# One pool of PSUM banks for the attention's products, 128-row products in the feature transform, and another instruction order

## The chip, the cores and the metric

The kernel runs on one core of a Trainium2 chip. The metric is the device time of one execution in microseconds (us), as a median of runs. TensorE (PE) multiplies, VectorE (DVE), ScalarE (ACT) and GpSimd (POOL) work element by element, SyncE (SP) issues most of the DMA transfers. PSUM, where TensorE's products arrive, has eight banks.

## The reference

Three stages follow each other, in fp32.

```python
# 1. attention: batch 4, heads 8, 768 steps, head size 40
for t in range(S):
    y[:, :, t] = einsum('bhd,bhde->bhe', rt, state)
    Sa = einsum('bhde,bhe->bhd', state, at)
    state = state * wt - einsum('bhd,bhe->bhde', Sa, bt) + einsum('bhd,bhe->bhde', vt, kt)
# 2. x = y as (4, 768, 320)
mixed = real(fft(fft(x, axis=1), axis=2)); u = x + mixed
un = (u - mean(u)) / sqrt(var(u) + 1e-6)
x = u + maximum(un @ w_ch1, 0) @ w_ch2                    # 320 -> 1280 -> 320
# 3.
h = maximum(x.T @ w_tok1, 0) @ w_tok2; u = x + h.T         # 768 -> 256 -> 768
out = u + maximum(u @ v1, 0) @ v2                          # 320 -> 1536 -> 320
```

## The kernel before, in words

**Attention** (class `Attn`). The 768 steps are cut into 12 chunks of 64 steps; 33 heads (one of them empty) lie in 11 groups of three. For each chunk VectorE makes running products of the decay (`decay`, scans at L293 and L296, reciprocal L295), TensorE makes `kg` (L328: products of the `k` and `b` rows with the masked `a` rows, 11 per chunk), and pairs of chunks go through the inversion of a triangular matrix on VectorE (`inv`, L366 to L381). The blocks for it are gathered through DRAM (`Gd`, then `N`), and its results go out to DRAM (`Md`, `Ad`) and come back turned round (`Mst`, `AT`). `merge` joins two half blocks by 32x32 products (`mg` L408, `mc` L418). Then the chain of a chunk runs on TensorE: `x` (L467), `z` (L479), `s` (L499); `s` makes the state with which the next chunk's `x` works. Off this chain lie `kbt` (L430) and `pt` (L447), turned copies of inputs, and the outputs: `zt` (L531), `st` (L523), `sc` (L538) and `y` (L556, L560). Each product lands in a PSUM bank, and ScalarE or VectorE copies it out (ScalarE's copies all have line 250).

**PSUM in the attention.** The eight banks are in five pools: `c` has two (chain and merge), `m` two (`kg`, `sc`), `t` two (turned copies), `y` one, `i` one (inversion). A product takes a bank of its pool and gives it back when its last copy is done.

**Feature transform.** The FFTs are products with tables. `fft` (L906, tile `psA`) goes along the steps, `fft2` (L929, tile `mix`) along the features. `fft2` has four groups per batch entry, 16 in all. Each group adds eight products in one bank: two of 384 columns and six of 192. Operands are split in a high and a low part; in `A[4]` the high part lies in partitions 0 to 63 and the low part in 64 to 127. The product with table 2 uses all 128 rows, the product with table 3 only the upper 64.

**MLPs.** For six blocks of 512 rows each, products `hps` (L998) and `acc` (L988) run over 10 hidden tiles in the first MLP and 12 in the second. `tok` and `tok2` (L1062, L1075) are the products along the steps.

**The order.** The kernel describes all work as operations with an engine, a cost, operands and banks. A planner (`emit`) puts them in an order: of the operations that can start soon it takes the one with the least due time; due times come from the costs, scaled by `SLACK`, plus a table of offsets `OFF` by stage and chunk. Each engine's order is fixed by that. Where the planner expects TensorE to wait for some time and a bank is free, it puts in fillers (`warm`, L59): products of a 128x128 identity that nobody reads. `HT` and the `cols` of an operation enter the planner's picture of TensorE's clock.

Of the kernel before, what the change touches and what calls it, by code (L numbers as in the profile page):

```python
# [19 lines left out]
NG,NH,D,L=11,33,40,64  # L20
NSC=768//L
T0,PERIOD=60,23.502442205459097
SLACK=453.4035
# [4 lines left out]
BANKS={'c': 2, 'm': 2, 't': 2, 'y': 1, 'i': 1}  # L28
YB='y'
# [181 lines left out]
class Attn:  # L211
# [107 lines left out]
    def kg(s,i):  # L319
# [3 lines left out]
        for g in range(0,NG,2):  # L323
            m=min(2,NG-g); w=192*m; h=s.psum('m',[128,512],"kg"); kp=('ps',h[0])
# [69 lines left out]
    def merge(s,i):  # L394
# [122 lines left out]
    def outp(s,i):  # L517
        nc=s.nc; P=s.P; LT=s.LT[i%2]; VZ=s.VZt; VZd=s.VZd; Sbd=s.Sbd; kbt=s.kbt[i%2]
        if i>0:
            h=s.psum('t',[128,512],"st"); kp=('ps',h[0])  # L520
# [6 lines left out]
        for g in range(0,NG,8):  # L527
            m=min(8,NG-g); hz=s.psum('t',[128,512],"zt"); kz=('ps',hz[0])
# [5 lines left out]
        for k in range(6):  # L534
            gs=(k,k+6) if k<5 else (k,); m=len(gs); hs=s.psum('m',[128,512],"sc"); ks=('ps',hs[0]); j=k%4; t=s.sc[j]
# [106 lines left out]
    def plan(s):  # L642
# [9 lines left out]
        s.P.op('NONE',0.0,lambda: None,pools=('y','t','m','c','i'))  # L652
# [16 lines left out]
OFF={'chain': -10683.5, ('chain', 0): -15631.6, ('chain', 1): -14799.7, ('chain', 10): 132022.4, ('chain', 11): 126346.1, ('chain', 2): -6299.2, ('chain', 3): -1037.2,  # L669
     ('chain', 4): 31922.7, ('chain', 5): 33526.1, ('chain', 6): 102034.8, ('chain', 7): 77429.7, ('chain', 8): 99749.8, ('chain', 9): 136807.5, 'dec2': -83569.5,  # L670
     ('dec2', 0): 207815.1, 'decay': -28442.6, ('decay', 0): -171758.2, ('decay', 1): -191635.0, ('decay', 10): 49032.8, ('decay', 11): 134393.3, ('decay', 2): -155857.3,
     ('decay', 3): -148976.4, ('decay', 4): -120978.7, ('decay', 5): 248332.4, ('decay', 6): -3537.5, ('decay', 7): 17076.9, ('decay', 8): 33468.6, ('decay', 9): 64147.4,
     'decode': 78098.6, ('decode', 0): 97303.6, 'fft': -34228.3, ('fft', 0): 157557.4, ('fft', 1): 148470.3, ('fft', 2): 199138.1, ('fft', 3): 189570.1,
     'fft2': -189107.1, ('fft2', 0): 311427.7, ('fft2', 1): 305214.4, ('fft2', 2): 353071.8, ('fft2', 3): 326784.8, 'inv': 58199.8, ('inv', 0): -246768.8,
     ('inv', 1): -80145.3, ('inv', 2): -56157.9, ('inv', 3): 18838.4, ('inv', 4): 54864.3, ('inv', 5): 54651.3, 'kbts': -115839.5, ('kbts', 0): -98283.9,
     ('kbts', 1): -98753.2, ('kbts', 10): 237625.0, ('kbts', 11): 239311.4, ('kbts', 2): 89305.9, ('kbts', 3): 103517.9, ('kbts', 4): 106114.8, ('kbts', 5): 137322.4,
     ('kbts', 6): 139123.4, ('kbts', 7): 199511.0, ('kbts', 8): 202633.2, ('kbts', 9): 224923.8, 'kg': -316699.4, ('kg', 0): 117017.4, ('kg', 1): 115337.6,
     ('kg', 10): 406897.7, ('kg', 11): 373952.9, ('kg', 2): 132794.7, ('kg', 3): 483438.3, ('kg', 4): 519031.2, ('kg', 5): 291674.5, ('kg', 6): 288959.4,
     ('kg', 7): 309931.9, ('kg', 8): 332304.5, ('kg', 9): 344543.4, 'load': -326373.5, ('load', 0): -39494.0, ('load', 1): 117623.2, ('load', 10): 338619.2,
     ('load', 11): 398123.7, ('load', 2): 115743.5, ('load', 3): 122285.7, ('load', 4): 112986.4, ('load', 5): 488502.3, ('load', 6): 478545.2, ('load', 7): 528238.0,  # L680
# [4 lines left out]
     'loada': -20378.0, ('loada', 0): -199541.7, ('loada', 1): -186254.8, ('loada', 10): 90123.2, ('loada', 11): 126291.1, ('loada', 2): -215592.5, ('loada', 3): -236036.9,  # L685
     ('loada', 4): 26756.8, ('loada', 5): 25194.9, ('loada', 6): 59786.8, ('loada', 7): 43065.6, ('loada', 8): 31025.7, ('loada', 9): 107881.0, 'merge': -133126.0,
     ('merge', 0): 302099.7, ('merge', 1): 296292.3, ('merge', 10): 276058.7, ('merge', 11): 274600.3, ('merge', 2): 105949.9, ('merge', 3): 133851.1, ('merge', 4): 151075.7,
     ('merge', 5): 149103.5, ('merge', 6): 220409.7, ('merge', 7): 222091.3, ('merge', 8): 248803.0, ('merge', 9): 242420.5, 'mlp': 37490.7, ('mlp', 0): 82923.3,
     ('mlp', 1): 140446.2, ('mlp', 10): 68410.7, ('mlp', 11): 66917.3, ('mlp', 2): -28738.2, ('mlp', 3): -39724.0, ('mlp', 4): 17549.8, ('mlp', 5): 147878.1,
     ('mlp', 6): 139739.8, ('mlp', 7): -8987.9, ('mlp', 8): 106168.0, ('mlp', 9): 82297.4, 'out_tile': 112459.4, ('out_tile', None): 28626.2, 'outp': -59596.5,  # L690
     ('outp', 0): 34493.1, ('outp', 1): 32964.5, ('outp', 10): 185593.1, ('outp', 11): 182730.1, ('outp', 2): 44389.6, ('outp', 3): 78826.9, ('outp', 4): 76975.8,
     ('outp', 5): 143298.3, ('outp', 6): 148343.4, ('outp', 7): 149927.6, ('outp', 8): 184311.6, ('outp', 9): 183929.4, 'pad': 66629.8, ('pad', 0): 52240.0,
# [488 lines left out]
```

## Time and profile before

| | us |
|---|---|
| median of 3 runs (lowest, highest) | 992.51 (989.52, 996.26) |
| profiled execution | 985.89 |
| its span, first to last instruction | 984.2 |
| TensorE busy | 956.7 |
| VectorE busy | 601.0 |
| ScalarE busy | 409.8 |
| GpSimd busy | 307.5 |

The span is the time on the chip between the first and the last instruction of the profiled execution; the profile's rows are from that execution. Busy time of TensorE counts the time from a product's start to its end in the pipeline, so products that overlap count once. PEld is TensorE's loading of weights, which goes on beside its products. A product of plain fp32 operands stands in the trace as two records for `kg`, `sc`, `x`, `y`, `mg` and the fillers among others. A wait is named by the instruction that ended it.

### The profile page before, as it was taken

To read this page: it belongs to the slowest core of one execution; us is meant where nothing else is said; L and a number is where in the kernel's file an instruction comes from. 1 tells how busy PE (TensorE), PEld (TensorE's weight loads), DVE (VectorE), ACT (ScalarE), POOL (GpSimd) and SP (SyncE) were. 2 spreads that over 40 slices of the span, in tenths; PEclk is the share of its full clock that TensorE was granted. 3 is DMA by queue.
4 is the path that set the end of the run, shared out by engine and by line. 5 is a ranking of instruction groups with operands and counts; after the bars stand their busy time and mean duration, and the time that the engine had idled before them with its cause. 6 is when DMAs were issued, how large, how long until landed. Compare 5 with 4: busy or idle time off the path is not lost.

```text
span 984.2 us, 23552 instructions
## 1 busy us (share of the span) xinstructions
PE 956.7 (97%) x9681; PEld 862.7 (88%) x9681; DVE 601.0 (61%) x1300; ACT 409.8 (42%) x830; POOL 307.5 (31%) x426
## 2 busy tenths in 40 slices
PE   9898999999899899999999999999999999999998
PEld 8898888888798788889888889899999898988987
DVE  5699679798888349989687646756244231312222
ACT  4366777877777465424343222324212121211111
POOL 6746437846743354021305433450000000000000
PEclk9999999999999899999999999999999999999999
DMA  9976679998786987251505553466000000000000
GB/s 226 192 180 157 153 189 219 189 224 201 192 193 164 218 234 249 104 156 43 161 17 178 155 156 106 157 222 232 1 1 28 1 27 1 27 1 28 1 28 27
DMA packets 128663, 123.93 MB, mean 126 GB/s; under 512 B 85119, under 2 KB 106059, under 8 KB 128555
## 3 DMA queue, kind: packets, MB, share of 16 engines
q1 hardware_dynamic: 123803, 100.39, 39.8%
q0 software_dynamic: 4752, 22.03, 6.5%
q8 instruction: 76, 1.25, 0.6%
q14 instruction: 32, 0.26, 0.1%
HBM read 83.76 MB, written 33.85 MB: 120 GB/s over the span
## 4 chain that ended last, share of the span: by engine, by line
PE 75%; DVE 11%; DMA 6%; POOL 3%; issue 2%; ACT 2%; SPq 1%; POOLq 0%; ACTq 0%; DVEq 0%
PE hps L998 24%; PE acc L988 22%; PE sc L538 4%; DVE pr L366 3%; PE kg L328 2%; PE warm L59 2%; PE mix L929 2%; PE tps L1062 2%; PE t2ps L1075 2%; PE y L560 2%; PE psA L906 2%; DVE Mt L367 2%; PE y L556 1%; PE trp L969 1%; DMA Mst<-Md 1%
## 5 line engine op out<-in xcount | busy, mean ns | idle before, releaser
L1001 DVE SCALAR_TENSOR_TENSOR hl<-hps,hh 128x512 fp32r<-128x512 f32 x132 | 91.1, 690 | 228.6 <-ACT hh L1000 228.4
L1000 ACT ACTIVATE hh<-hps 128x512 fp32r<-128x512 f32 x132 | 78.9, 598 | 322.7 <-PE hps L998 322.5
L998 PE MATMUL hps<-th,v 128*128 128x512 f32 x432 | 135.2, 396 | 0.0
L988 PE MATMUL acc<-v,hh 128*128 128x320 f32 x576 | 128.6, 310 | 0.0
L998 PE MATMUL hps<-th,W 128*128 128x512 f32 x360 | 112.5, 396 | 0.4 <-DVE th L974 0.3
L988 PE MATMUL acc<-W,hh 128*128 128x320 f32 x480 | 107.6, 311 | 0.0
L988 PEld LDWEIGHTS acc<-v,hh 128*128 128x128 f32 x576 | 98.4, 188 | 5.1
L852 POOL TENSOR_TENSOR mda<-mda,mdh 128x320 f32<-128x320 f32 (+2 forms) x44 | 45.3, 1042 | 183.1 <-DVE mdt L850 159.2
L998 PEld LDWEIGHTS hps<-th,v 128*128 128x128 f32 x432 | 81.1, 188 | 16.7
L988 PE MATMUL acc<-v,hl 128*128 128x320 f32 x288 | 88.9, 309 | 0.0
L59 PE MATMUL warm<-ident 128*128 128x128 f32 x664 | 85.6, 283 | 2.0 <-POOL Q L254 2.0
L988 PEld LDWEIGHTS acc<-W,hh 128*128 128x128 f32 x480 | 81.6, 188 | 3.7
L59 PEld LDWEIGHTS warm<-ident 128*128 128x128 f32 x664 | 79.7, 196 | 3.6 <-POOL Q L254 2.0
L998 PEld LDWEIGHTS hps<-th,W 128*128 128x128 f32 x360 | 67.7, 188 | 14.8 <-PE trp L969 0.5
L988 PE MATMUL acc<-W,hl 128*128 128x320 f32 x240 | 74.3, 310 | 0.3 <-DVE hl L1001 0.3
L998 PE MATMUL hps<-tl,v 128*128 128x512 f32 x144 | 57.0, 396 | 0.0
L538 PE MATMUL sc<-rm,VZd 120*128 120x192 f32 x264 | 54.9, 342 | 1.9 <-DVE sc L543 1.0
L988 PEld LDWEIGHTS acc<-v,hl 128*128 128x128 f32 x288 | 54.1, 188 | 0.0
L328 PE MATMUL kg<-am,bt 120*128 120x192 f32 x242 | 50.7, 353 | 3.2 <-ACT am L250 2.3
L328 PEld LDWEIGHTS kg<-am,bt 120*128 120x128 f32 x242 | 41.2, 201 | 7.7 <-POOL bt L305 2.5
L998 PE MATMUL hps<-tl,W 128*128 128x512 f32 x120 | 47.3, 394 | 0.0
L538 PEld LDWEIGHTS sc<-rm,VZd 120*128 120x128 f32 x264 | 41.6, 189 | 6.3 <-DVE sc L543 2.6
(179 smaller groups left out, 1947.8 us busy)
## 6 DMA issues: line engine op xcount, KB each, us to landing
bt<-in_bkR_dram SPq DMA_DIRECT2D x12, 660.0 KB
mdraw<-in_moe_w_ch_dram SPq DMA_DIRECT2D x22, 320.0 KB
wS<-in_wR_dram SPq DMA_DIRECT2D x12, 335.2 KB
a<-in_aR_dram SPq DMA_DIRECT2D x12, 335.2 KB
RT<-a SPq DMA_DIRECT2D x36, 111.7 KB
LT<-in_vT_dram SPq DMA_DIRECT2D x12, 330.0 KB
VZt<-in_vT_dram SPq DMA_DIRECT2D x12, 330.0 KB
r<-in_rR_dram SPq DMA_DIRECT2D x12, 330.0 KB
```

Source lines behind the costliest of these rows:

```text
L59: for x in range(m): nc.tensor.matmul(t[:,128*(x%4):128*(x%4)+128],lhsT=ident,rhs=ident,start=True,stop=True)
L328: nc.tensor.matmul(ps[:,192*x:192*x+192],lhsT=bt[:,g+x].rearrange("p v t -> p (v t)"),rhs=am[:,:,g+x],start=True,stop=True)
L366: P.op('DVE',(.02+.0022*st[0]*shape[0]) if shape[0]==4 and shape[1]<8 else (.048+.00108*st[0]*shape[0]),lambda: V.tensor_tensor(out=pr,in0 ...
L367: P.op('DVE',c,lambda: V.tensor_reduce(out=ev(o),in_=pr,axis=AX.X,op=ALU.add),[('pr',h)],wr)
L538: for x,g in enumerate(gs): nc.tensor.matmul(ps[:,192*x:192*x+192],lhsT=VZd[:,g].rearrange("p v t -> p (v t)"),rhs=s.rm[:,:,g],start=True, ...
L560: nc.tensor.matmul(ps[64*x:64*x+64,c:c+40],lhsT=t[:,3*x+hh],rhs=kbt[:,3*g+hh],start=i==0,stop=True,skip_group_check=True)
L852: P.op('POOL',.06+d*.0025,lambda: nc.gpsimd.tensor_tensor(out=g("da").bitcast(F32),in0=g("da").bitcast(F32),in1=g("dh").bitcast(F32),op=AL ...
L906: nc.tensor.matmul(ps[:,c0:c0+cn],lhsT=t[xx][:,k,o:o+128],rhs=s.at.T1[:,r,tb,c0:c0+cn],start=n==0 and g==0,stop=n==len(seq)-1 and g==len(G)-1)
L988: nc.tensor.matmul(s.pst(acc[x]),lhsT=a[:,sl],rhs=t[w2][w][:,m],start=(m==0 and n==0),stop=(m==MT-1 and n==2))
L998: for n,(l,r) in enumerate(ops): nc.tensor.matmul(ps,lhsT=l,rhs=r,start=n==0,stop=n==7)
L1000: s.act(512,lambda: nc.scalar.activation(out=t["hh"][z],in_=s.pst(h),func=AF.Relu),[kp],[('hh',z)],free=[h[0]])
L1001: s.dve(.61,lambda: nc.vector.scalar_tensor_tensor(out=t["hl"][z],in0=s.pst(h),scalar=0.0,in1=t["hh"][z].bitcast(F32),op0=ALU.max,op1=ALU. ...
```

## The change

All products of the attention take their bank from one pool `c` of seven banks; `i` keeps one. In the transform along the features the product with table 3 uses all 128 rows; the lower half of table 3, zero before, now repeats its upper half. The `cols` of the two 32x32 products of `merge` are 307 instead of 512, `HT` is 3550 instead of 3300, `SLACK` 1446.5 instead of 453.4, and the whole table `OFF` has other numbers (the diff shows a line of it).

```diff
-SLACK=453.4035
+SLACK=1446.5000
-BANKS={'c': 2, 'm': 2, 't': 2, 'y': 1, 'i': 1}
-YB='y'
+BANKS={'c': 7, 'i': 1}
+YB='c'
...
-            m=min(2,NG-g); w=192*m; h=s.psum('m',[128,512],"kg"); kp=('ps',h[0])
+            m=min(2,NG-g); w=192*m; h=s.psum('c',[128,512],"kg"); kp=('ps',h[0])
...
-            P.op('PE',.255,f,[('B',i%4),('AT',i%4)]+([kp+(0,)] if k else []),[kp+(k,),('T',32),('T',96)],alloc=h[0] if k==0 else None,cols=512,ni=32,q='D')
+            P.op('PE',.255,f,[('B',i%4),('AT',i%4)]+([kp+(0,)] if k else []),[kp+(k,),('T',32),('T',96)],alloc=h[0] if k==0 else None,cols=307,ni=32,q='D')
...
-            h=s.psum('t',[128,512],name); kp=('ps',h[0])
+            h=s.psum('c',[128,512],name); kp=('ps',h[0])
...
-            gs=(k,k+6) if k<5 else (k,); m=len(gs); hs=s.psum('m',[128,512],"sc"); ks=('ps',hs[0]); j=k%4; t=s.sc[j]
+            gs=(k,k+6) if k<5 else (k,); m=len(gs); hs=s.psum('c',[128,512],"sc"); ks=('ps',hs[0]); j=k%4; t=s.sc[j]
...
-OFF={'chain': -10683.5, ('chain', 0): -15631.6, ('chain', 1): -14799.7, ('chain', 10): 132022.4, ('chain', 11): 126346.1, ('chain', 2): -6299.2, ('chain', 3): -1037.2,
+OFF={'chain': -74749.0, ('chain', 0): 150606.4, ('chain', 1): 226254.3, ('chain', 10): 223225.9, ('chain', 11): 231718.6, ('chain', 2): -17036.4, ('chain', 3): 110610.3,
...
-HT=3300.0
+HT=3550.0
...
-    T2[64:,2]=T2[:64,2]
+    T2[64:,2:]=T2[:64,2:]
...
-                ops=[(A[4],2,128,W),(A[4],3,64,W)]+[y for e in range(2) for y in ((A[2*e],0,128,E[e]),(A[2*e],1,128,E[e]),(A[2*e+1],0,128,E[e]))]
+                ops=[(A[4],2,128,W),(A[4],3,128,W)]+[y for e in range(2) for y in ((A[2*e],0,128,E[e]),(A[2*e],1,128,E[e]),(A[2*e+1],0,128,E[e]))]
```

**First place: TensorE, from behind the first chunk's `x` to the first `mc`.** `kg` names the chunk by its operand (`bt_124`, `bt_125` and `bt_122` are chunks 2, 3 and 4). Before:

```order
L328 MATMUL kg<-am_117,bt_124 128x192 x11
L59 MATMUL warm<-ident 128x128 x19
L328 MATMUL kg<-am_117,bt_125 128x192 x4
L59 MATMUL warm<-ident 128x128 x2
L328 MATMUL kg<-am_117,bt_125 128x192 x4
L59 MATMUL warm<-ident 128x128
L328 MATMUL kg<-am_117,bt_125 128x192 x3
L59 MATMUL warm<-ident 128x128 x54
L328 MATMUL kg<-am_117,bt_122 128x192 x11
L59 MATMUL warm<-ident 128x128 x11
L408 MATMUL mg<-AT_145,B_146 32x32 x32
L59 MATMUL warm<-ident 128x128 x6
```

With the change:

```order
L328 MATMUL kg<-am_117,bt_124 128x192 x11
L59 MATMUL warm<-ident 128x128 x19
L328 MATMUL kg<-am_117,bt_125 128x192 x11
L59 MATMUL warm<-ident 128x128 x69
L328 MATMUL kg<-am_117,bt_122 128x192 x11
L408 MATMUL mg<-AT_145,B_146 32x32 x32
L59 MATMUL warm<-ident 128x128 x14
L418 MATMUL mc<-Mst_143,T_147 32x32 x32
```

The products are the same; the fillers go from 93 to 102 here, and `mg` follows `kg` directly.

**Second place: the queue of SP and VectorE around the first inversion.** `Gd_157` takes the blocks of chunks 0 and 1 (`RT_131`, `RT_132`), `N_118` reads them back, `wS` and `bt` are loads for later chunks. SP before:

```order
L248 DMA Gd_157<-RT_131 32x32x32 x2
L248 DMA bt_122<-in_bkR_dram 120x1408
L248 DMA bt_125<-in_bkR_dram 120x1408
L248 DMA RT_131<-a_115 40x715 x3
L248 DMA Gd_157<-RT_132 32x32x32 x2
L248 DMA wS_110<-in_wR_dram 120x715
L248 DMA N_118<-Gd_157 64x1024
L248 DMA a_115<-in_aR_dram 120x715
L248 DMA RT_132<-a_116 40x715 x3
L248 DMA N_118<-Gd_157 64x1024
```

With the change:

```order
L248 DMA bt_125<-in_bkR_dram 120x1408
L248 DMA Gd_157<-RT_131 32x32x32 x2
L248 DMA VZd_141<-in_vR_dram 120x11x64
L248 DMA r_138<-in_rR_dram 120x704
L248 DMA N_118<-Gd_157 64x1024
L248 DMA Gd_157<-RT_132 32x32x32 x2
L248 DMA RT_131<-a_115 40x715 x3
L248 DMA wS_110<-in_wR_dram 120x715
L248 DMA N_118<-Gd_157 64x1024
```

The second `N` now stands behind three `RT` and one `wS` after `Gd`, without the load of `a_115` and the three `RT_132`. On VectorE, inside the inversion (`Mt`, `pr`, `it`), there stood before:

```order
L366 TENSOR_TENSOR pr_121<-N_118,it 128x512 x2
L367 TENSOR_REDUCE it<-pr_121 128x8x8 x2
L366 TENSOR_TENSOR pr_121<-Mt_119,it 128x512 x2
L367 TENSOR_REDUCE Mt_119<-pr_121 128x8x8 x2
L381 COPY it<-Mt_119 128x256
```

And with the change:

```order
L367 TENSOR_REDUCE it<-pr_121 128x8x8 x2
L366 TENSOR_TENSOR pr_121<-Mt_119,it 128x512 x2
L367 TENSOR_REDUCE Mt_119<-pr_121 128x8x8 x2
L293 SCALAR_TENSOR_TENSOR Q_112<-wS_111,D_113 120x715
L295 RECIPROCAL D_114<-Q_112 120x11
L296 SCALAR_TENSOR_TENSOR R_126<-wS_111,D_114 120x715
L381 COPY it<-Mt_119 128x256
```

The two scans and the reciprocal of chunk 5 moved into the inversion; a reciprocal and a scan of chunk 4 (`R_130`), which stood ahead of it, moved in as well, near its start.

**Third place: TensorE around the chain of chunk 5.** Before:

```order
L479 MATMUL z<-bdX_142,Mst_144 64x80 x16
L430 MATMUL kbt<-ident,bt_124 128x120 x4
L328 MATMUL kg<-am_117,bt_123 128x192 x4
L430 MATMUL kbt<-ident,bt_124 128x120 x4
L328 MATMUL kg<-am_117,bt_123 128x192 x4
L430 MATMUL kbt<-ident,bt_124 128x120 x3
L328 MATMUL kg<-am_117,bt_123 128x192 x3
L499 MATMUL s<-VZt_137,kbt_149 40x40 x33
L531 MATMUL zt<-ident,VZt_137 120x64 x11
L59 MATMUL warm<-ident 128x128 x10
L467 MATMUL x<-LT_135,RT_133 64x40 x32
```

With the change:

```order
L328 MATMUL kg<-am_117,bt_123 128x192 x11
L408 MATMUL mg<-AT_145,B_146 32x32 x32
L59 MATMUL warm<-ident 128x128 x10
L418 MATMUL mc<-Mst_144,T_147 32x32 x32
L59 MATMUL warm<-ident 128x128 x5
L479 MATMUL z<-bdX_142,Mst_144 64x80 x16
L59 MATMUL warm<-ident 128x128 x5
L499 MATMUL s<-VZt_137,kbt_149 40x40 x33
L531 MATMUL zt<-ident,VZt_137 120x64 x11
L59 MATMUL warm<-ident 128x128 x5
L538 MATMUL sc<-rm_140,VZd_141 128x192 x6
```

`kbt` and `kg` products, which stood between `z` and `s`, stand ahead of `mg`; between the links of the chain there are fillers.

## Rows read from the trace of the kernel before

**Rows 1.** The page's head: span, then busy us, share and instructions of each engine.

```profile
span 984.2 us, 23552 instructions
...
PE 956.7 (97%) x9681; PEld 862.7 (88%) x9681; DVE 601.0 (61%) x1300; ACT 409.8 (42%) x830; POOL 307.5 (31%) x426
```

**Rows 2.** By stretch: length, busy time of each engine, clock, DMA share, GB/s.

```profile
0.00:75.00 75.00, 69.94 (x592) 67.65 (x593) 54.60 (x81) 36.58 (x56) 46.46 (x71) 0.98 0.86 201
75.00:390.00 315.00, 298.38 (x5666) 264.81 (x5664) 244.89 (x538) 218.83 (x437) 174.44 (x260) 0.98 0.81 196
390.00:425.00 35.00, 33.34 (x224) 28.45 (x223) 32.30 (x100) 15.97 (x51) 3.91 (x4) 1.00 0.41 145
425.00:984.20 559.20, 555.01 (x3206) 501.80 (x3205) 269.25 (x583) 138.46 (x290) 82.65 (x92) 1.00 0.23 75
```

**Rows 3.** TensorE's waits from 75 to 390: us in total, times, longest.

```profile
PE mc L418 <- ACT T L250: 4.0, 2, 3.7
...
PE pt L447 <- ACT kbt L250: 1.1, 1, 1.1
```

**Rows 4.** Timeline of TensorE: start, length, instructions; fillers and what follows.

```profile
63.85 12.22 PE L59 MATMUL warm<-ident 128*128 128x128 f32 x108
...
75.91 4.45 PE L328 MATMUL kg<-am,bt 120*128 120x192 f32 x22
```

**Rows 5.** Groups by form; a wait of the weight loads; pieces of the chain.

```profile
L929 PE MATMUL mix<-T,A 64*128 64x384 f32 x16 | 7.0, 438 | 0.0
...
L929 PEld LDWEIGHTS mix<-T,A 64*128 64x128 f32 x16 | 2.9, 183 | 3.5 <-issue 3.5
...
PEld mix L929 <- issue: 6.5, 32, 0.3
...
425.87 1.87 PE hps L998 x8
...
430.90 2.79 PE mix L929 x16
...
491.64 4.02 PE psA L906 x36
```

**Rows 6.** Timeline of TensorE at 120 us: `mg` and what follows it.

```profile
120.51 0.44 PE L408 MATMUL mg<-AT,B 32*32 32x32 f32 x16
120.88 0.63 PE L430 MATMUL kbt<-ident,bt 120*128 120x120 f32 x4
121.44 0.95 PE L408 MATMUL mg<-AT,B 32*32 32x32 f32 x48
122.32 0.53 PE L430 MATMUL kbt<-ident,bt 120*128 120x120 f32 x3
```

**Rows 7.** Groups by form: weight loads of `sc` and `kg`, idle time before them.

```profile
L538 PEld LDWEIGHTS sc<-rm,VZd 120*128 120x128 f32 x264 | 41.6, 189 | 6.3 <-DVE sc L543 2.6 <-issue 0.9 <-ACT sc L250 0.9
L328 PEld LDWEIGHTS kg<-am,bt 120*128 120x128 f32 x242 | 41.2, 201 | 7.7 <-POOL bt L305 2.5 <-ACT RT L250 1.8 <-issue 1.8
```

**Rows 8.** Pieces of the chain, 0 to 80 us: start, length, what.

```profile
30.37 7.62 DMA Gd<-RT
...
40.41 6.50 DMA N<-Gd
```

**Rows 9.** Timeline of VectorE: a scan, a reciprocal, the inversion's first and last.

```profile
35.12 1.65 DVE L293 TENSOR_TENSOR_SCAN Q<-wS,D 120x715 f32<-120x715 f32 x1 [5.28 <-POOL R L299]
36.80 0.23 DVE L295 RECIPROCAL D<-Q 120x11 f32<-120x11 f32 x1
...
47.41 0.17 DVE L369 COPY Mt<-it 128x4 f32<-128x4 f32 x1 [0.97 <-ACT it L368]
...
69.22 1.21 DVE L367 TENSOR_REDUCE Mt<-pr 128x32 f32<-128x512 f32 x2
```

**Rows 10.** A piece of the chain, and the stretch behind it (columns of rows 2).

```profile
317.53 11.29 DMA AT<-Ad
...
336.35:343.15 6.80, 6.62 (x164) 6.33 (x166) 1.16 (x4) 3.01 (x7) 0.86 (x1) 0.50 0.71 193
```

More of the change, by code (lines that the diff above doesn't have):

```diff
@@ L418, in f @@
                     nc.tensor.matmul(ps[p:p+32,n//2],lhsT=s.T[p+32:p+64,n//2],rhs=Mst[p+32:p+64,n//2,32:64],start=True,stop=True,skip_group_check=True)
-            P.op('PE',.255,f,[('T',32),('T',96)]+D+([kq+(0,)] if k else []),[kq+(k,),('Mst',x,2)],alloc=g[0] if k==0 else None,cols=512,ni=32,q='D')
+            P.op('PE',.255,f,[('T',32),('T',96)]+D+([kq+(0,)] if k else []),[kq+(k,),('Mst',x,2)],alloc=g[0] if k==0 else None,cols=307,ni=32,q='D')
         for p in (0,64):
@@ L443, in pts @@
             gs=[(k-k0,x,k+6*x) for k in range(k0,k0+kn) for x in range(2) if k+6*x<NG]
-            h=s.psum('t',[128,512],"pt"); kp=('ps',h[0])
+            h=s.psum('c',[128,512],"pt"); kp=('ps',h[0])
             def f(gs=gs,h=h):
@@ L519, in outp @@
         if i>0:
-            h=s.psum('t',[128,512],"st"); kp=('ps',h[0])
+            h=s.psum('c',[128,512],"st"); kp=('ps',h[0])
             def f():
@@ L527, in outp @@
         for g in range(0,NG,8):
-            m=min(8,NG-g); hz=s.psum('t',[128,512],"zt"); kz=('ps',hz[0])
+            m=min(8,NG-g); hz=s.psum('c',[128,512],"zt"); kz=('ps',hz[0])
             def f(g=g,m=m,hz=hz):
@@ L651, in plan @@
         s.P.filler=lambda b,j,m: warm(s.nc,s.ps[b][j],s.ident,m)
-        s.P.op('NONE',0.0,lambda: None,pools=('y','t','m','c','i'))
+        s.P.op('NONE',0.0,lambda: None,pools=('c', 'i'))
         go(0,'load'); s.init(); go(0,'decay','kg','loada'); s.init2(); first(1); s.init3()
@@ L668 @@
 BL=2.761166073747128
-OFF={'chain': -10683.5, ('chain', 0): -15631.6, ('chain', 1): -14799.7, ('chain', 10): 132022.4, ('chain', 11): 126346.1, ('chain', 2): -6299.2, ('chain', 3): -1037.2,
[L670 to L680, printed above, removed]
[4 rows of a table removed]
[L685 to L692, printed above, removed]
-     'pts': -65642.9, ('pts', 0): -153885.4, ('pts', 1): 39076.5, ('pts', 10): 190183.7, ('pts', 11): 178987.4, ('pts', 2): 58178.1, ('pts', 3): 53924.8,
-     ('pts', 4): 85782.3, ('pts', 5): 85106.6, ('pts', 6): 153334.9, ('pts', 7): 143312.5, ('pts', 8): 151428.5, ('pts', 9): 188736.7, 'tok': -290701.5,
-     ('tok', 0): 472044.2, ('tok', 1): 464667.7, ('tok', 2): 437332.8, ('tok', 3): 428210.6, 'tok2': -443306.7, ('tok2', 0): 679101.0, ('tok2', 1): 602125.0,
-     ('tok2', 2): 565845.0, ('tok2', 3): 417967.0, 'wdec': 108931.7, ('wdec', 0): 35575.6, ('wdec', 1): 38674.8, ('wdec', 10): -299.7, ('wdec', 11): 4844.7,
-     ('wdec', 2): -152569.0, ('wdec', 3): -138466.9, ('wdec', 4): -102678.7, ('wdec', 5): -100979.8, ('wdec', 6): -31010.7, ('wdec', 7): -25950.9, ('wdec', 8): -46380.3,
-     ('wdec', 9): -2547.4}
@@ L1114, in finish @@
         for x in (s.m3s,s.w2s,s.left,s.k2s): x.close()
-PA=('c','c','i')
+PA=('c', 'c', 'i')
 TM=343.0758349479737
```

25 lines of the change are left out of this document (added), and 8 rows, old and new, of the table OFF.

## The prediction

> **What bounds the kernel now.** I read the page's first section, then the busy time by stretch, then the waits of TensorE. TensorE is busy for 956.7 of 984.2 us [rows 1], so the sum below is made in TensorE time, and the reader is to see where that time could shrink. By stretches [rows 2] there are two regimes. From 425 us to the end TensorE is busy for 555.0 of 559.2 us: the two MLPs stream product after product and whatever is taken from a product there comes off the end. In the 390 us before, TensorE sits idle for 5.1 us (0 to 75) and 16.6 us (75 to 390), while VectorE is busy for 245 of the 315 us, ScalarE for 219 and the DMA engines for 81%. No engine fills that stretch; it is held together by waits of one engine for another. The fillers (`warm`, products of the identity whose result nobody reads) stand where the plan expected TensorE to wait. The longest TensorE wait named there is 4.0 us for the evacuation of `mg` [rows 3].
>
> The profiled execution took 985.89 us for a span of 984.2 (1.7 around it); the median of the runs is 992.51, 0.7% above. I make the sum against 984.2 and move the median by the same number of microseconds.
>
> **The change, part by part.**
>
> *Fillers.* Counted in the two orders, TensorE's products other than fillers are the same 6397; the fillers grow from 332 to 408. Each is two records. From the first of 108 records to the product behind them pass 75.91 - 63.85 = 12.06 us [rows 4], so a filler costs 0.223 us. By place: ahead of the first `mc` 219 become 244 (+25, 5.6 us); from there to the first `mix` 84 become 140 (+56, 12.5 us); after that 29 become 24 (-5, -1.1 us). All 76 together are 17.0 us. They cost that if TensorE has work it could do instead, and nothing where it would have waited anyway.
>
> *The 64-row product.* Each of the 16 groups of `mix` has eight products, of which one has 64 rows. Two groups take 2.79 us, so one takes 1.395 [rows 5]. What should it take? A product of 512 columns takes 1.87/8 = 0.233 us (`hps`), one of 192 takes 4.02/36 = 0.112 (`psA`), and one of 384, by its columns, 0.174. Two of 384 and six of 192 make 1.02 us. So 0.375 us a group goes elsewhere, and the row of the weight loads says where: they sat idle 32 times, twice in each of 16 groups, for 6.5 us in total, and waited for nothing that the profile shows [rows 5]. Half of it stands before the 64-row load itself (3.5 us over 16). I read this as the price of going to 64 rows and back. With 128 rows in all eight, 16 x 0.375 = 6.0 us go. Twelve of the groups stand between MLP products, where TensorE never waits, and come off the end in full (4.5 us). The first four stand ahead of the first MLP product, on the path to it, but with fillers beside them; I count them too. Bounds: 0, if the second 384-column product is slow for another reason, and 6.5, the idle time itself. I take 6.0. The extra 64 rows add no columns, and the table's lower half is filled on the host into the same transfer.
>
> The Trainium skill, "TensorEngine Tiling (Array Packing)", Tiling Modes (Key Properties), says that going from one tiling mode to another drains the engine; the 0.2 us beside each of the 32 loads agrees. Against it, "TensorE: Matmul & The Clock Gate", Part 2 (LDWEIGHTS), says that a load's time goes with its columns and that the row count doesn't matter; by that alone the edit is worth nothing and the sum ends 6 us higher, which is the third rival below.
>
> *Changes of shape.* The attention's products come in four shapes (128 or 120 rows by 120 or 128 columns; fewer columns; 40 or 64 rows; 32 by 32). Eight `mg` products and the change behind them take 120.88 - 120.51 = 0.37 us, 24 of them 122.32 - 121.44 = 0.88 [rows 6]; so a product takes 0.032 and the change 0.115. In the order before TensorE goes from shape to shape 229 times, in the new one 208 times: -21 x 0.12 = -2.5 us.
>
> *One pool of banks.* `kg` and `sc` shared two banks and now share seven with everything else. What this can give is the time that their weight loads waited for an evacuation [rows 7]: for `kg` 1.8 us (ScalarE's `RT`), for `sc` 2.6 (VectorE) and 0.9 (ScalarE), 5.3 us; with the 1.1 us that `pt` waited for `kbt`'s evacuation among TensorE's waits, 6.4. Bounds 0 and 6.4. I take half of 5.3, -2.7, because the evacuations are no faster and later products still need their results.
>
> *The new order, start.* The first `mc` waits for the first inversion, and that for `N`. Before, its last transfer is issued at 40.41 us and takes 6.5 [rows 8]; between the landing of `Gd` (37.99) and that issue SP's queue spent 2.4 us on three `RT` transfers and what lay between. In the new order these three and the load of `wS` stand ahead while `Gd` is under way, so `N` may leave at once: -2.4 us, up to -5 with two loads fewer ahead of it. Against this, VectorE now does three scans and two reciprocals inside the inversion, which took from 47.41 to 70.43 us by itself [rows 9]: 3 x 1.65 + 2 x 0.23 = 5.4 us. Behind the inversion, `AT` is issued with one load between it and the writing of `Ad`, where before five transfers lay between. I put the start at +1.0 us, between -2 and +5.6 (all its fillers).
>
> *The new order, attention.* Fillers +12.5 us. The third order fence shows why: the chain `mg`, `mc`, `z`, `s`, `zt` of one chunk, which had `kg` and `kbt` products between its links, now has fillers between them. They take TensorE time, but some of it is time in which it waited before: of 16.6 us idle [rows 2], I let a third of the new fillers, 4.2 us, stand in such waits, for the plan foresees only a part of them. It does not foresee the worst: the transfer of `AT` that took 11.3 us, behind which TensorE then ran for 6.8 us at a granted clock of 0.50 [rows 10], 1.2 GHz instead of 2.4. In the new queue a load of `VZd` again stands ahead of that `AT`.
>
> Sum: -6.0 (64 rows) +1.0 (start) +12.5 -4.2 (fillers in the attention) -2.5 (shapes) -2.7 (banks) -1.1 (fillers later) = -3.0 us. The profiled span would be 981.2, the median 989.5.
>
> **The rivals.**
>
> *The fillers simply add.* If TensorE's waits in the attention stay as long as they are (they are set by landings and evacuations, not by banks), the fillers come on top: +5.6 +12.5 -1.1 -2.5 -6.0 = +8.5 us, 1001.0. For it speaks that in the new order dependent products stand closer (the `z` of the last chunk directly behind its `x`), so that a late evacuation is no longer hidden. It decides from the point where TensorE, between 75 and 390 us of work, still idles 16 us or more.
>
> *The waits go.* If the shared banks give their full 6.4 us, half of the new fillers stand in old waits (another -2.1) and the late `AT` of 317 us is in time (4.0 us of wait and half of 6.8 us at half clock, -7.4), the sum is -3.0 -3.7 -2.1 -7.4 = -16 us, 976.
>
> *The doubled rows bring nothing.* Then -3.0 + 6.0 = +3.0, 995.5. Against it speaks the idle time before exactly those loads.
>
> **How the numbers follow.** My forecast (982 to 998 by itself) has a chance of 0.50, fillers that add (998 to 1008) 0.25, waits that go (970 to 982) 0.19, rows that bring nothing 0.06. The predicted time is 989.5. The range from 976 to 1004 leaves out about 0.1 on each side. About 1% (9.9 us) is what a measurement of this kernel can tell from no change. Faster by over 1% (below 982.6) takes the third case and a little of the first: 0.23. Slower by over 1% (above 1002.4) takes under the better half of the fillers that add, and a little of the late start: 0.17. The rest, 0.60, is within 1%.
>
> **What would show it.** `mix` groups of about 1.0 us, and weight loads there without idle time, show the 6.0 us right; groups of 1.4 us show it wrong. The first `mc` starts at 85.4 us now; at 84 to 88 the start is as I put it. Idle time of TensorE from 75 to 390 us near 10 us, with some 30 us of fillers there, shows the fillers in waits; idle of 16 us or more shows that they added. The first `hps` starts at 416.0 us now; it should start at about 417.5 (the sum without the twelve groups behind it), and from there to the end 4.5 us less than the 568.2 of now should pass. The forecast is wrong above all if the late transfers of the attention come at other places: a wait of 4 us costs its half clock as well.

## The result and the profile after

The changed kernel takes 980.33 us (median of 4 runs, 973.90 to 983.35) beside 991.01 us for the kernel before on the same chip: a ratio of 0.9894, with a 95% interval of 0.9853 to 0.9935. The forecast was 989.5, range 976 to 1004, most of the chance on "within 1%". The range holds the time; the forecast itself was 9 us too long, and the change came out at the edge between "same" and "faster by 1%". The experiments brought nineteen more runs of the changed kernel and, beside them and the others, 96 of the kernel before. The means of the 23 and of the 96 are 981.7 and 990.3 us, so the change is worth **-8.6 us (95%: 1.7 either way)**, where the sum had -3.0.

The page of the changed kernel begins with its span, and then the busy time of each engine (answers to [rows 1]):

```profile
span 972.2 us, 23884 instructions
...
PE 952.2 (98%) x9833; PEld 873.1 (90%) x9833; DVE 604.3 (62%) x1300; ACT 409.9 (42%) x830; POOL 305.8 (31%) x426
```

By stretch, in the columns of [rows 2]:

```profile
0.00:75.00 75.00, 71.35 (x627) 69.97 (x628) 53.51 (x82) 34.66 (x52) 50.54 (x73) 1.00 0.89 203
75.00:390.00 315.00, 304.65 (x5826) 278.36 (x5825) 248.37 (x555) 225.34 (x457) 168.54 (x255) 0.99 0.82 203
390.00:425.00 35.00, 33.07 (x219) 29.50 (x218) 32.79 (x97) 13.32 (x36) 9.31 (x10) 1.00 0.31 97
425.00:972.20 547.20, 543.14 (x3168) 495.32 (x3166) 269.65 (x571) 136.58 (x287) 77.39 (x88) 1.00 0.23 76
```

TensorE idles for 10.4 us between 75 and 390 us, where it idled for 16.6 [rows 2]. What it still waits for there (total, times, longest; answers to [rows 3]):

```profile
PE kg L328 <- POOL bt L305: 2.1, 2, 1.0
PE y L560 <- POOL sc L548: 1.5, 2, 0.8
PE s L499 <- ACT VZt L250: 1.5, 2, 0.9
PE mc L418 <- issue: 1.4, 2, 1.3
```

The wait of 4.0 us of `mc` for `T` is gone, and nothing longer than 1.3 us stands in its place in this profile; two more profiles of the changed kernel have waits of up to 2.4 us (`s` for `VZt`), and none of `mc` for `T`. The forms of `mix` and the weight loads of `sc` and `kg` (answers to [rows 5, 7]):

```profile
L538 PEld LDWEIGHTS sc<-rm,VZd 120*128 120x128 f32 x264 | 42.0, 190 | 1.3 <-issue 0.2
L328 PEld LDWEIGHTS kg<-am,bt 120*128 120x128 f32 x242 | 39.0, 190 | 3.8 <-POOL bt L305 2.5 <-ACT am L250 0.8 <-issue 0.2
...
L929 PEld LDWEIGHTS mix<-T,A 128*128 128x128 f32 x128 | 17.6, 190 | 2.1 <-issue 0.7 <-ACT DE L932 0.7 <-DVE tl L973 0.5
...
L929 PE MATMUL mix<-T,A 128*128 128x384 f32 x32 | 8.6, 350 | 1.2 <-DVE DE L933 0.7 <-DVE tl L973 0.3 <-issue 0.2
```

There is no form of 64 rows any more, and the 6.5 us in which the weight loads of `mix` waited for nothing are 0.7. The weight loads of `sc` and `kg` idle for 5.1 us where they idled for 14.0. In the chain of waits, one group of `mix` takes 1.01 us (eight products in the first line), where it took 1.395 [rows 5]:

```profile
430.01 1.01 PE mix L929 x8
431.01 1.88 PE hps L998 x8
434.66 2.02 PE mix L929 x16
```

**How the runs are compared.** The two profiled executions are 12.0 us apart in span (984.2 and 972.2), the means of all runs only 8.6. What the two profiles have on top is mostly TensorE's clock. The profile after has a mean granted clock of 0.998, about the highest of its 23 runs (their mean is 0.9917); the profile before has 0.991, where the mean of its 96 runs is 0.9877. In the stretches below 1, TensorE is granted 1.2 GHz in place of 2.4, as in [rows 10]. They come and go from execution to execution of one and the same kernel. Every run lists its span and its mean clock, so the two can be put beside each other: over the 221 runs of all kernels here, each kernel against its own mean, a clock lower by 0.001 goes with a span longer by 0.785 us (0.065 either way). A clock lower by 0.001 means about 2 us more at half speed, which would cost 1 us if TensorE were all that counts, so four fifths of it is paid. With that slope each kernel's mean span splits into a span at full clock and a part that the clock costs. The runs come from several chips; at full clock the kernel before takes between 978.5 and 979.2 us on each of the four that ran the experiments, so they are put together. The split is an estimate: differences of spans at full clock are good to about 1 to 1.8 us, and to 2.5 to 2.8 for the two kernels without fillers, whose clocks (0.951 to 0.962) lie below those of all other runs (0.976 to 0.998), so that the slope is carried beyond most of what it was measured on. Seven more runs, each over 1.5% longer than the fastest of its kernel, are left out of the slope and the table; with them the slope is 0.84 us.

| kernel | runs | mean us | mean clock | span at full clock, us |
|---|---|---|---|---|
| before | 96 | 990.3 | 0.9877 | 978.9 |
| changed | 23 | 981.7 | 0.9917 | 973.5 |
| mix128_b | 12 | 984.8 | 0.9878 | 973.6 |
| mix64_a | 10 | 987.0 | 0.9914 | 978.5 |
| pool_b | 11 | 987.9 | 0.9869 | 975.9 |
| pool_mix_b | 11 | 983.7 | 0.9862 | 971.2 |
| mru_a | 12 | 989.8 | 0.9869 | 977.8 |
| thin_a | 10 | 984.1 | 0.9836 | 969.5 |
| nofill_a | 6 | 998.2 | 0.9563 | 962.2 |
| nofill_b | 6 | 1006.8 | 0.9573 | 971.3 |
| more_a | 12 | 987.1 | 0.9910 | 978.3 |
| more_pm | 12 | 990.0 | 0.9861 | 977.4 |

The whole change is thus -5.4 us at full clock and -3.2 us of clock.

### The profile page after: what moved, and what is told of

The parts are those of the page before. It is cut to its first block, busy times and chain, and to the rows that moved or that the text cites. A ratio compares the mean times of both kernels' runs of the same rounds, so it can differ in the third digit from the quotient of the medians.

```text
span 972.2 us, 23884 instructions
## 1 busy us (share of the span) xinstructions
PE 952.2 (98%) x9833; PEld 873.1 (90%) x9833; DVE 604.3 (62%) x1300; ACT 409.9 (42%) x830; POOL 305.8 (31%) x426
## 4 chain that ended last, share of the span: by engine, by line
PE 75%; DVE 9%; DMA 7%; ACT 3%; issue 2%; POOL 2%; SPq 1%; DVEq 0%; POOLq 0%; ACTq 0%
PE hps L998 24%; PE acc L988 23%; PE warm L59 4%; PE kg L328 3%; PE sc L538 3%; PE t2ps L1075 2%; PE tps L1062 2%; PE trp L969 2%; DMA a<-in_aR_dram 1%; PE y L560 1%; DVE pr L366 1%; PE z L479 1%; SPq L248 1%; PE s L499 1%; PE mg L408 1%
## 5 line engine op out<-in xcount | busy, mean ns | idle before, releaser
L59 PE MATMUL warm<-ident 128*128 128x128 f32 x816 | 103.4, 283 | 2.0 <-POOL Q L254 2.0
L59 PEld LDWEIGHTS warm<-ident 128*128 128x128 f32 x816 | 97.2, 196 | 3.6 <-POOL Q L254 2.0
L998 PEld LDWEIGHTS hps<-th,v 128*128 128x128 f32 x432 | 81.1, 188 | 16.6
L998 PEld LDWEIGHTS hps<-th,W 128*128 128x128 f32 x360 | 67.6, 188 | 14.2 <-issue 0.4
L853 POOL TENSOR_TENSOR mda<-mda,mdt 128x320 fp32r<-128x320 f32 (+2 forms) x44 | 42.2, 966 | 41.7 <-DVE q L950 22.9
L538 PE MATMUL sc<-rm,VZd 120*128 120x192 f32 x264 | 51.3, 336 | 0.0
L548 POOL TENSOR_SCALAR_AFFINE_SELECT sc<-sc 64x384 f32<-64x384 f32 (+1 forms) x72 | 37.6, 525 | 38.8 <-ACT sc L250 36.4
L305 POOL TENSOR_TENSOR bt<-bt,Q 120x512 f32<-120x512 f32 (+1 forms) x33 | 39.7, 1224 | 26.3 <-PE warm L59 12.5
```

Source lines behind the costliest of these rows:

```text
L59: for x in range(m): nc.tensor.matmul(t[:,128*(x%4):128*(x%4)+128],lhsT=ident,rhs=ident,start=True,stop=True)
L305: en.tensor_tensor(out=o,in0=o,in1=view(Q,(L+1)*g+2,[L+1,m],[0,2],[1,L]),op=ALU.mult)
L538: for x,g in enumerate(gs): nc.tensor.matmul(ps[:,192*x:192*x+192],lhsT=VZd[:,g].rearrange("p v t -> p (v t)"),rhs=s.rm[:,:,g],start=True, ...
L548: nc.gpsimd.affine_select(out=o,in_=o,pattern=[[0,3*m],[-1 if i in ROW else 1,L]],compare_op=ALU.is_gt,fill=0.0,base=L-1 if i in ROW else ...
L853: P.op('POOL',.06+d*.0025,lambda: nc.gpsimd.tensor_tensor(out=g("da").bitcast(F32R),in0=g("da").bitcast(F32),in1=g("dt").bitcast(F32),op=A ...
L998: for n,(l,r) in enumerate(ops): nc.tensor.matmul(ps,lhsT=l,rhs=r,start=n==0,stop=n==7)
```

## The experiments

The first reading of the two profiles gave a theory that the runs then had to bear: the shared banks made most of the gain. Between the profiles, the starts of `kg`'s products had moved from 0.41 to 0.35 us apart and those of `sc` from 0.40 to 0.37, over 132 products each some 12 us, and the banks were what had changed for them. The rival was that the new order and its fillers had made the gain.

**The 128-row product alone, and its undoing.** mix128_b is the kernel before with this edit, and mix64_a is the changed kernel with it taken back:

```diff
-    T2[64:,2]=T2[:64,2]
+    T2[64:,2:]=T2[:64,2:]
-                ops=[(A[4],2,128,W),(A[4],3,64,W)]+...
+                ops=[(A[4],2,128,W),(A[4],3,128,W)]+...
```

> The kernel before with one edit: the eight groups of the feature transform read 128 rows in the product that read 64. Order, banks and fillers as before. If the 64-row products cost what the prediction says (0.093 + 0.190 + 0.092 us over a 128-row one, sixteen times), it is 6.0 us shorter than the kernel before, a ratio of about 0.994, and the mix groups take about 1.0 us each with no idle time of their weight loads. Rival: the transform has slack beside it and the gain is given back before the end; then ratio 0.998 to 1.002 with the same short groups.

> The changed kernel with the 64-row products put back in the feature transform, all else kept. By the prediction's price it is 6.0 us longer than the changed kernel: a ratio of about 0.995 to the kernel before where the changed one has 0.989. Rival: the new order hides it, and the ratio stays at 0.989.

mix128_b is at 0.9947 of the kernel before (0.9925 to 0.9970): -5.5 us, of which -5.3 at full clock. mix64_a is 5.3 us longer than the changed kernel, 5.1 of it at full clock (1.7 either way). The two agree with each other and with the 6.0 of the sum. The forms of `mix` in mix128_b (first line) and in mix64_a show that it is the 64-row loads and the change around them:

```profile
L929 PEld LDWEIGHTS mix<-T,A 128*128 128x128 f32 x128 | 17.6, 190 | 1.3 <-issue 0.6 <-DVE tl L973 0.4
```

```profile
L929 PEld LDWEIGHTS mix<-T,A 128*128 128x128 f32 x112 | 14.5, 190 | 4.2 <-issue 3.4 <-DVE tl L973 0.5 <-ACT A L918 0.2
...
L929 PE MATMUL mix<-T,A 64*128 64x384 f32 x16 | 7.0, 439 | 0.0
...
L929 PEld LDWEIGHTS mix<-T,A 64*128 64x128 f32 x16 | 2.9, 183 | 3.5 <-issue 3.5
```

The idle time of 3.4 and 3.5 us, waiting for nothing that the profile shows, returns with the 64-row loads and goes with them. The rival, that slack beside the transform takes the gain back, falls.

**Shared banks in the old order, and fresh banks in the new one.** pool_b keeps the planned order of before with its division of banks, and its fillers, word for word; only the bank that a product really gets is chosen among all seven, the one free longest. pool_mix_b has the 128-row product besides. mru_a keeps the order and the fillers of the changed kernel and takes, in place of the bank free longest, the one that came free last:

```diff
+        real={(b,j):0.0 for b,n in BANKS.items() if b!='i' for j in range(n)}; s.real={}
...
                 f=free[h[0]]; j=f.index(min(f)); s.bank[h]=j; f[j]=1e9
+                if h[0] in BANKS and h[0]!='i': k=min(real,key=real.get); s.real[h]=k; real[k]=1e9
```

In mru_a the choice is `max((k for k,x in real.items() if x<=t),key=real.get)`.

> The kernel before with its planned order and its fillers word for word, but each product of the attention takes, among the seven banks outside the inversion, the one that has been free longest, in place of the one of its own kind. Nothing else moves. The prediction's term for this was -2.7 us (bounds 0 and 6.4). Theory after the result: the products of kg and sc stop waiting on evacuations that have just ended, worth about 0.05 us for each of 264 products, 10 to 13 us in all, a ratio of 0.987 to 0.990; the start-to-start time of kg's products falls from 0.41 towards 0.35 us. Rival: the new order made the gain, and this gives 0 to 3 us, a ratio of 0.997 to 1.0.

> Both edits together in the order of before: shared banks and 128-row products, 24 to 56 fillers fewer than the changed kernel in each stretch. Theory (banks 10 to 13, mix 6, new order and its fillers give back about 5 of it): 16 to 19 us shorter than before, a ratio of 0.981 to 0.984, so faster than the changed kernel. Rival (order made the gain): 6 to 9 us, a ratio of 0.991 to 0.994.

> The changed kernel with its order and fillers word for word, but each product of the attention takes the free bank that was evacuated last, in place of the one free longest. No product is placed where the planner saw no free bank. Theory (fresh banks cost the waits): 8 to 13 us longer than the changed kernel, a ratio of 0.998 to 1.003 to the kernel before, and kg's products start 0.40 us apart again in place of 0.35. Rival (the order made the gain, which bank is taken does not matter): ratio 0.989 as the changed kernel.

pool_b is at 0.9969 (0.9941 to 0.9997): -2.4 us, -3.0 at full clock. This is the -2.7 of the forecast and not the 10 to 13 of the theory made after the result, which falls. pool_mix_b is at 0.9929 (0.9897 to 0.9962), -6.5 us, where that theory wanted 16 to 19; at full clock it is 7.7 us shorter than before, 2.4 shorter than mix128_b (1.6 either way). The weight loads of pool_b (six lines were added above, so `sc` is on line 544 and `kg` on 334) show where it comes from:

```profile
L334 PEld LDWEIGHTS kg<-am,bt 120*128 120x128 f32 x242 | 43.6, 210 | 6.3 <-POOL bt L311 5.2 <-issue 0.4
L544 PEld LDWEIGHTS sc<-rm,VZd 120*128 120x128 f32 x264 | 42.1, 191 | 2.3 <-issue 1.0
```

And the loads of `kg` in mru_a (first line) and in a second profile of the changed kernel (after_again):

```profile
L334 PEld LDWEIGHTS kg<-am,bt 120*128 120x128 f32 x242 | 38.9, 190 | 3.8 <-POOL bt L311 2.3 <-issue 0.5 <-ACT Sbd L256 0.4
```

```profile
L328 PEld LDWEIGHTS kg<-am,bt 120*128 120x128 f32 x242 | 40.8, 197 | 2.8 <-POOL bt L305 2.4 <-issue 0.2
```

The idle time of `sc`'s loads falls from 6.3 [rows 7] to 2.3 us, and the waits for VectorE and ScalarE are off the row; `kg`'s falls from 7.7 to 6.3, and what is left there is the wait for `bt`, which no bank changes. So the visible idle time for evacuations (5.3 us) held as a bound. The closer starts of `kg` in the first profile after were no matter of banks either: taken from the traces, with gaps over 0.8 us left out, they are 0.41 us before and 0.39 in pool_b, where the theory had it fall towards 0.35, and 0.34 in the changed kernel and in mru_a, where it wanted 0.40. They belong to the order. Nor does the mean time of a load tell of banks: it is 210 ns in pool_b, but it is also 197 in after_again and 190 in the first profile after, which are the same kernel at mean clocks of 0.986 and 0.998.

In the new order, too, the choice of bank counts: mru_a is at 0.9994 (0.9966 to 1.0022), 8.1 us longer than the changed kernel, 4.3 at full clock and the rest clock (0.9869 against 0.9917). Always taking the freshest of seven banks is another choice than the small pools of before, so its price can't be set against that of pool_b. Its waits of TensorE from 75 to 390 us show three that no other profile of a kernel with this order has, all for `ys`, the evacuation of a bank of `y`:

```profile
PE y L562 <- DVE ys L582: 2.0, 1, 2.0
...
PE pt L453 <- DVE ys L582: 0.6, 2, 0.3
PE kbt L436 <- DVE ys L582: 0.5, 1, 0.5
```

The three together are 3.1 us, beside 4.3 at full clock. Why the clock is lower too is not shown.

**The changed kernel again.** The first profile after had hardly any slow clock. Was that the change, or the one execution?

> The changed kernel itself beside the three others on one chip: 0.985 to 0.994 of the kernel before by the first measurement, with a second profile to see whether the slow stretches of TensorE's clock (four of about 3.4 us before, one in the first profile after) are part of the change or of the single execution. If they belong to the execution, this profile shows two to four of them and a span near 978 us.

> The changed kernel once more. By the eleven runs so far it is 8.5 to 10 us shorter than the kernel before, a ratio of 0.990 to 0.992, with a mean granted clock near 0.992 against 0.987. If its higher clock was chance, the clock comes out at 0.986 to 0.988 and the ratio at 0.994 to 0.996.

The ratios are 0.9927 (0.9891 to 0.9963) and 0.9934 (0.9905 to 0.9963). Both profiles are slower than the first (spans of 985.5 and 980.3 us at clocks of 0.986 and 0.991), so the 12 us between the first two profiles were part luck. The span of 985.5 lies above the 978 that the expectation named, and the ratio of after_3 between the two cases of its own, with a clock (0.991) that speaks for the first. But over all runs the clock of the changed kernel is still higher than that of the kernel before, 0.9917 (standard error 0.0009) against 0.9877 (0.0004), and the four kernels with the order and fillers of before all lie between 0.986 and 0.988. So 3.2 us of the gain are clock, and come with the new order and its fillers. These alone don't make it: mru_a, with the same order and fillers, is at 0.9869.

**Fewer fillers.** thin_a keeps the order of the changed kernel and takes two of five fillers out of the attention, and a few just ahead of it; nofill_a takes all of them out from the last one ahead of the first chunk on to the transform. nofill_b does to the kernel before what nofill_a does to the changed one:

```diff
+            if 75<t<375: m=(3*m+2)//5
-            if not DRY: s.filler(*b,m)
+            if not DRY and m: s.filler(*b,m)
```

(in nofill_a and nofill_b `m=0`). Counted in the orders, 59 fillers go in thin_a, 154 in nofill_a and 101 in nofill_b.

> The changed kernel with fillers thinned from 140 to 87 in the attention (84 before) and from 244 to 238 ahead of it; the order of all other work is kept. If the extra fillers added their time, as the rival of 1001 us had it, 53 fillers of 0.223 us fewer make it 12 us shorter, a ratio of 0.977 to the kernel before. If they stand in waits that are there anyway, it is the same within 2 us (0.987 to 0.991), or longer where the granted clock falls in the attention without them.

> The changed kernel with no filler at all between the first chunk and the transform (140 fewer), the order of other work kept. Fillers that add: 31 us shorter. Fillers in waits with no use: same within 2 us. Fillers that hold the clock: more stretches with a granted clock of 0.5 in the attention, each about 1.7 us lost, so 3 to 10 us longer.

> The kernel before without its 84 fillers in the attention and the last 17 ahead of the first chunk, the order of other work kept. It asks whether fillers have the same price and the same use in the old order. Theory: 0.07 us each is saved at full clock (7 us), and the clock pays for it as it did in the changed kernel, where 154 fillers held up 28 us: some 18 us here, a mean granted clock near 0.965, together 9 to 13 us longer, a ratio of 1.009 to 1.013. Rival: the fillers of the old order stand where they hold no clock, since two more in each run bought none; then the clock stays at 0.986 to 0.988 and it is 5 to 7 us shorter, a ratio of 0.993 to 0.995.

thin_a is at 0.9938 (0.9906 to 0.9971), 2.4 us longer than the changed kernel (3.5 either way), and not 12 shorter. nofill_a, which was expected to be 3 to 10 us longer if fillers hold the clock, is at 1.0079 (1.0053 to 1.0105) and nofill_b at 1.0159 (1.0110 to 1.0209): both 16.6 us longer with less work. The stretch from 75 to 390 us (columns of [rows 2]) of thin_a, nofill_a and nofill_b:

```profile
75.00:390.00 315.00, 298.00 (x5631) 270.14 (x5629) 238.93 (x509) 218.25 (x426) 165.58 (x252) 0.94 0.78 188
```

```profile
75.00:390.00 315.00, 282.33 (x5372) 256.23 (x5371) 231.57 (x491) 215.63 (x420) 159.40 (x240) 0.89 0.78 183
```

```profile
75.00:390.00 315.00, 285.67 (x5377) 253.56 (x5376) 235.70 (x497) 216.64 (x420) 166.89 (x247) 0.90 0.80 189
```

The clock of the stretch is 0.94, 0.89 and 0.90, against 0.99, 0.96 and 0.97 in three profiles of the changed kernel and 0.98 [rows 2] in that of the kernel before. So a filler does two things, and the table parts them. At full clock, thin_a is 3.9 us shorter than the changed kernel, nofill_a 11.2, and nofill_b 7.6 shorter than the kernel before: 0.067, 0.073 and 0.075 us for each filler gone (0.02 to 0.03 either way; with the slope of 0.84 us they would be 0.070, 0.086 and 0.093). Of its 0.223 us [rows 4] a third is paid, and two thirds stand in waits that are there anyway, in either order. Against this, the clock pays 6.4, 27.8 and 24.2 us: 0.11, 0.18 and 0.24 us for each. Nothing of the expectation that a filler adds its whole time is left, and of nofill_b's two theories the one that gives fillers the same price and use in the old order holds, with more clock lost (0.957) than it put.

**More fillers.** more_a adds two fillers to each run of fillers of the attention in the changed kernel (56 more), more_pm does the same to pool_mix_b (46 more):

```diff
+            if 75<t<375: m+=2
             if not DRY: s.filler(*b,m)
```

> The changed kernel with two fillers more in each of its 28 runs of fillers between the first chunk and the transform (196 in place of 140); the order of all other work is kept. Theory: a run of fillers as long as the planned wait costs 0.07 us a filler and buys clock, one that is longer than the wait costs its whole 0.22 us; so 12 us are added, and at most 6.5 us of clock can come back: 5 to 10 us longer than the changed kernel, a ratio of 0.996 to 1.002. Rival: fillers cost a third wherever they stand and the clock rises with them: 4 us added, 3 to 5 back, the same as the changed kernel, 0.990 to 0.993.

> The order of before with shared banks and 128-row products, and two fillers more in each run in the attention (126 in place of 84, and 4 more ahead of it). Without them that kernel stood at 0.993 with a clock of 0.986. Theory (whole 0.22 us beyond the wait): 10 us added, 2 to 5 us of clock back, a ratio of 0.997 to 1.002. Rival (a third wherever they stand): 3 us added, 4 back, 0.991 to 0.993.

more_a is at 0.9972 (0.9943 to 1.0001), 5.4 us longer than the changed kernel, more_pm at 1.0013 (0.9985 to 1.0041), 6.3 us longer than pool_mix_b. At full clock they pay 0.086 and 0.136 us for each filler, and neither gains any clock: 0.9910 after 0.9917, and 0.9861 after 0.9862. So the theory was right that fillers beyond the planned wait don't pay, and both ratios lie in its ranges, but by luck: the price is below its 0.22 us, and the clock that it let come back did not come. None of the kernels here has a lower mean than the changed one; pool_mix_b and thin_a are shorter at full clock and give it back in clock. But the changed kernel is only 2.1 us below pool_mix_b (2.9 either way): the 128-row product and the shared banks alone, in the order of before, give 6.5 of the 8.6 us, and what the new order and its fillers add to that in time can't be told from nothing.

## Why the prediction was right and wrong

*The 64-row product: right.* -6.0 forecast, -5.3 in the old order (1.1 either way), -5.1 in the new. Groups take 1.01 us, as forecast. From the first `hps` to the end, three profiles of the changed kernel take 562.6, 563.2 and 563.7 us where 568.2 passed before: 5.0 less, 4.5 forecast. The Trainium skill, "TensorEngine Tiling (Array Packing)", Tiling Modes (Key Properties), has the change of mode drain the engine. The runs agree: the 3.5 us of idle time before the sixteen 64-row loads of mix64_a are not there in mix128_b. The Trainium skill, "TensorE: Matmul & The Clock Gate", Part 2 (LDWEIGHTS), says that the row count doesn't matter for a load: the load itself bears that out (183 ns with 64 rows, 190 with 128, in mix64_a), but the edit that would then be worth nothing is worth 5.1 to 5.3 us, since the price lies beside the loads.

*The banks: right.* -2.7 forecast; -3.0 alone (1.2 either way), -2.4 on top of the 128-row product. The bound of 5.3 us was read from waits; that half of it would come was a choice, and the interval would have borne anything from a third to four fifths. The Trainium skill, "Perfetto Trace Analysis", Optimizing Tensor Performance (Matmuls), says that independent groups of products should rotate through the PSUM banks, so that one's evacuation lies beside the next one's products. The runs agree: pool_b gains 3.0 us and mru_a loses 4.3 at full clock.

*The start: not decided.* The first `mc` starts at 86.5, 85.3 and 86.3 us in three profiles of the changed kernel; in the profiles of before, mix128_b, pool_b and pool_mix_b it starts at 85.4, 87.5, 87.8 and 87.0. The test "at 84 to 88" is met by all of them, with either order, so it can't tell the +1.0 from nothing; its sign is not settled. The first `hps`, forecast at 417.5, starts at 409.6, 422.3 and 416.6 in the three profiles.

*The fillers in the attention: the step that failed.* The sum let a third of the new ones stand in old waits ("I let a third of the new fillers, 4.2 us, stand in such waits") and charged 12.5 - 4.2 = 8.3 us for 56 of them, 0.148 each. Three kernels with fewer fillers or none show 0.067 to 0.075 each, so 56 cost some 3.9 us: it is about two thirds that stand in waits. The plan foresees its waits better than the sum gave it credit for. Its test in the trace was the idle time between 75 and 390 us, "near 10", and it came out at 10.4 in the first profile, but at 14.2 and 12.2 in the other two, so it could not have told a third from two thirds; the runs with fewer fillers do.

*The clock: a term that the sum did not have.* It took fillers as a cost only, and the slow clock of [rows 10] as something that a late transfer brings. But the fillers hold the clock up: taken out, they lose 1.6 to 3.2 times as much in clock as they cost. The changed kernel gets 3.2 us from a clock that is higher by 0.004.

*The wait of `mc`: gone as a rival had it, but not for its reason.* The prediction put the wait of 4.0 us of `mc` for `T` down to the 11.3 us transfer of `AT` [rows 10]. The sum kept it, since a load of `VZd` stands ahead of that `AT` again; the rival "the waits go" had the `AT` in time. The waits of `mc` for `T` from 75 to 390 us, in mix128_b and in pool_b, which have the old order:

```profile
PE mc L418 <- ACT T L250: 4.0, 2, 3.7
```

```profile
PE mc L424 <- ACT T L256: 4.2, 2, 3.9
```

and those of `mc` and `mg` in the last profile of the changed kernel:

```profile
PE mc L418 <- issue: 1.9, 2, 1.5
...
PE mg L408 <- DMA AT<-Ad: 0.6, 1, 0.6
```

But in the profile of before, `mg`, which reads `AT`, ran in time, directly behind `x`. What came late is ScalarE's copy `T` (timeline; in brackets the engine's idle time before it):

```profile
329.74 1.20 PE L408 MATMUL mg<-AT,B 32*32 32x32 f32 x64
...
334.78 0.47 ACT L849 ACTIVATE mdh<-mda 128x320 fp32r<-128x320 f32 x1 [4.69 <-DVE mda L848]
...
335.27 1.20 ACT L250 ACTIVATE T<-mg 32x512 f32<-32x512 f32 x2
```

And in the first profile of the changed kernel:

```profile
329.25 0.59 ACT L250 ACTIVATE T<-mg 32x512 f32<-32x512 f32 x1
...
334.40 0.47 ACT L849 ACTIVATE mdh<-mda 128x320 fp32r<-128x320 f32 x1
```

`mdh` is a step in the preparation of the MLP weights. In ScalarE's old order it stood ahead of the two copies `T` and waited 4.69 us for VectorE's `mda`, in turn made from a load of these weights (4.76 us in mix128_b, 4.73 in pool_b); in the new order the copies stand ahead of `mdh`. So it is ScalarE's order that removed the wait, and not the transfer of `AT`, as far as traces can show it; no run moved `mdh` alone. The wait is gone in all three profiles of the changed kernel, and `mc` waits 1.4 to 2.0 us there for other things, so 2.0 to 2.6 us are gained. Of the slow clock behind it some is left: TensorE runs at 0.50 for 3.4, 6.8 and 3.4 us there, where it was 6.8, 10.2 and 10.2 in before, mix128_b and pool_b.

*The changes of shape:* -2.5 forecast, and not measured by itself. pool_mix_b and the changed kernel have the same banks and products and differ in order and fillers alone: +2.3 us at full clock (1.4 either way). 76 fillers at 0.07 are +5.3, which leaves -3.0 for the order, and that holds the wait of `mc`, the start and the changes of shape together. How it divides stays open.

So the account is: -5.3 (128 rows) -2.4 (banks) +5.3 (fillers) -3.0 (order, by difference) -3.2 (clock) = -8.6 us. Order and fillers together were put at +1.0 +8.3 -2.5 -1.1 = +5.7; they are +2.3 and -3.2 of clock. That is where the missing 6 us are. What also stays open is why the old order gains no clock from 46 fillers more (more_pm) while the new one holds 0.004 more than the old. It may be that the place of a filler counts and not the number, but no run here moved fillers at equal count.

The chances missed in the same place. "Fillers that add" had 0.25 and "waits go" 0.19; the truth lies between the forecast and "waits go", of which the wait of `mc` went (by another cause) and more fillers stood in waits, while the larger gain from banks did not come. "Within 1%" had 0.60 for a change of 0.9%.

## What to carry to other kernels

Fillers have a price and a use, and neither is their busy time: take them out and put them back once, in a kernel of its own, and read the span against the mean granted clock of each run, before charging them in a sum. One profile against another compares two executions, and where the clock moves between executions of one kernel, as it does here by 0.015, a gain read from two profiles is first set beside the clocks of all runs. A product of 64 rows inside a group of 128-row products was worth filling up here, at about 0.33 us for each. And a wait is read back on the engine that ended it: what stood ahead of the late copy in that engine's own order may be the cause, and not the longest transfer near it.

## What the runs showed of the hardware

In these kernels TensorE, busy for 282 of 315 us without fillers in the attention, is granted a mean clock of 0.89 over that stretch; with 140 fillers, busy for 301 to 305 in three profiles, it is granted 0.96 to 0.99; with 196 fillers, busy for 307, 0.97. 16.6 us of 982 hang on products whose result nobody reads. A 64-row product among 128-row ones cost about 0.33 us, while its load took no longer than theirs (183 and 190 ns). Two fillers more in each run bought no clock in either order. And the same program's mean clock ranged from 0.983 to 0.998 over 23 executions, with spans from 972.2 to 987.1 us: at one level of work the clock is not a constant of the kernel.
